# Query projections in 64-row halves beside scores in block 0, in cycles of three pairs, and the output weight's parts in DRAM

## The chip, the cores and the metric

The kernel runs on one core of a Trainium2 chip. The time is that of one launch on the device in microseconds (us); three runs of the kernel before gave 1419.66 to 1421.75, median 1420.86. The engines that matter here: PE (TensorE, matrix products), ACT (ScalarE, the exponentials), DVE (VectorE, elementwise work, and copies out of PSUM), POOL (GpSimd, weight preparation) and SP (SyncE, which issues most DMAs). Each works through a queue of its own in program order, and semaphores join them.

## What is computed

One transformer block on x of 2048 tokens by 512. There are 32 query heads of 16 columns that share one key and one value head; the feed-forward part has 1792 hidden columns.

```python
q = ln(x) @ wq                    # 32 heads of 16
k, v = ln(x) @ wk, ln(x) @ wv     # one head of 16
p = softmax(q @ k.T * 16**-0.5)   # each head: 2048 x 2048
h = x + concat_heads(p @ v) @ wo
h2 = h + (gelu(ln(h) @ w_gate) * (ln(h) @ w_up)) @ w_down
```

Every product with a weight is made of three products of split operands: high part by high part, low by high, high by low.

## The kernel before

Tokens are worked in four **blocks** of 512 (b = 0 to 3). In a block, eight **groups** of four heads (g) run over 16 **key chunks** of 128 keys (kc). The unit of the loop is a **pair** n: two heads of one key chunk. Two pairs make a chunk, 32 pairs a group, 256 pairs a block.

For a pair, `scores` (L361) issues two matmuls, one on the upper and one on the lower half of PE's rows (50 rows used in each: the query's high and low parts, and a bound for the exponent), into a score buffer `s` of two PSUM banks, and one exp of 128x1024 on ACT (L372). Three score buffers rotate in the stage in question, so pair n can't be scored before the exp of pair n-3 is done. When both pairs of a chunk have their exps, `weigh` (L374) multiplies the four heads' probabilities by v and a column of ones, in four column tiles of 32 (16 MATMUL rows of the trace are two chunks), into one accumulator `acc`. After 16 chunks `evacuate` (L387) copies it to SBUF on DVE (`oT`, L389), stores it to DRAM (`acc_d`, L393) and loads it back in another layout (`oc`, four DMAs, L402). When two groups are back, DVE takes reciprocals, divides, and splits the result into `o_hi` and `o_lo` (L414 to L433). Those steps wait in a list, `outs`, and `take_out` (L383) issues one entry of it now and then. In block 0 four empty entries are put ahead of them, so that they come later; with the last group of the block all entries are issued at once.

While block 0's scores run, the queries of the later blocks are still to be projected. `project_q` (L184) makes a block's queries in four parts c of 128 columns: 12 matmuls of 128x128x512 (L194) into `pq`, which has one buffer. DVE then reads `pq` for `qh` and `ql` (L116, L117), SP stores them to `q_d`, from which `load_q` (L349) takes each group's queries some time ahead. A block's last part is followed by four small matmuls for the squared norms (`pqn`, L232), and two steps on DVE (L236, L237). From these `factors` (`mm`, L242 to L251, on POOL) and `bound` (`m`, L258 on DVE, then a DMA) make the bound. After the last block's, `check_bound` stores a few numbers to `b_d` (L1387).

POOL meanwhile prepares the weights in `part_weights` (L466): 46 steps of load, split into high and low part, and store to DRAM; wo's four steps leave their parts in SBUF instead (L474).

The order of all this is written out by hand, in the loop `while n < lead` (L1014 to L1042); `lead` is 272. Every fourth pair is preceded by one step of the projections (three matmuls, L1024 to L1027), then four pairs are complete and all chunks but the last two pairs' are weighed (`finish`, L1035), an entry of `outs` is taken (L1037) and a step of the weight parts (L1039). When the projections are done, one chunk is weighed after every second pair (L1030). SP and DVE keep the order of the program in this stretch.

At n = 256 the pools of the first stage are closed. At n = 260 the dense part of block 0 is primed (`dense(0)`, L575): two loads of x (`xb`, L583) and the first four weight loads (`w1`, 512 KB each, L528), whose memory was that of the first stage. From n = 272 on its matmuls are woven among the scores of block 1, the output projection first (`project`, in 64-row halves by `duo`, L548). That projection runs over c = 0 to 3, and the last, c = 3, needs the eighth group's result. Later blocks repeat this, and a tail (L691) ends the last.

Of the kernel before, what the change touches and what calls it, by code (L numbers as in the profile page):

```python
# [9 lines left out]
F32 = mybir.dt.float32  # L10
F32R = mybir.dt.float32r
# [24 lines left out]

HURRY = ((0, 3), (1, 0), (1, 1))
# [7 lines left out]
CUT, EDGE, GAP, HOLD = -1, -2, -3, -4  # L45
# [3 lines left out]
def kernel(  # L49
# [51 lines left out]
    wo_hi = const.tile([P, DC, D], F32R, name="wo_hi")  # L101
    wo_lo = const.tile([P, DC, D], F32R, name="wo_lo")
# [7 lines left out]
    w2_d = dram.tile([FC, P, 2, D], F32R, name="w2_d")  # L110

# [43 lines left out]
    def run(outer, first):  # L155
# [28 lines left out]
        def project_q(b, cs, eng, col):  # L184
# [4 lines left out]
            for c in cs:  # L189
                pq = psum1(f"pq_{b}_{c}")  # L190
                n = 0
                for d in range(DC):
                    for wt, xt in ((wq_hi, xT_hi), (wq_hi, xT_lo), (wq_lo, xT_hi)):
                        nc.tensor.matmul(  # L194
                            pq, wt[:, d, c * P : (c + 1) * P], xt[:, d, :],
                            start=(n == 0), stop=(n == 3 * DC - 1),
                        )
                        n += 1
                    if urgent or d < DC - 1:
                        yield 3  # L200
# [72 lines left out]
            yield 2  # L273
# [19 lines left out]

        def later_products():
            second = project_q(1, range(DC), nc.vector, 1)
# [4 lines left out]
            for _ in range(2 * DC - sum(RAMP.values())):  # L300
                yield next(second)
            yield from q_rest
            yield from second
            for b in range(2, NB):
                yield from project_q(b, range(DC), nc.vector, b)

        def first_q():

            qg = eb.tile([P, 2, T], F32R, name="qg_first")
            view = q_d.rearrange("(u a) r s -> a r u s", a=2)  # L310
# [264 lines left out]
        def dense(b, tail=False):  # L575
# [15 lines left out]
            if b == 0:  # L591
                yield 0
# [872 lines left out]
```

## Time and profile before

| | |
|---|---|
| median of three runs | 1420.86 us (1419.66 to 1421.75) |
| the profiled execution | 1419.23 us, of which the profile's span is 1417.5 us |
| granted TensorE clock, mean | 0.998 |
| first exp of pair n = 32 / 256 / 271 | 85.69 / 307.55 / 321.30 us |
| first matmul of the output projection (`pp`) | 323.26 us |

Times in the profile count from the start of its span. Two executions differ by some tenths of a per cent, so terms that are worked out from the trace are put on the profiled execution's own time, and the median stands beside it. In a row of a time line, the first number is the start, the second the length, then engine, line of the program, operation, result, sources, shapes and count; in brackets stands the engine's idle time before it, and whose work ended that. Matmul rows overlap: the start of the next one tells when PE went on.

### The profile page before, as it was taken

The numbers are of one execution on the slowest core, as the hardware profiler recorded it, in microseconds if no ns is written. First come the engines' busy times: TensorE is split into PE (matmuls) and PEld (weight loads), VectorE is DVE, ScalarE is ACT, GpSimd is POOL, SyncE is SP. The second block draws the span as 40 slices with busy tenths as digits, with TensorE's granted clock in tenths as the row PEclk, the third lists the DMA queues.
The fourth block names the chain that finished last, engine by engine and source line by source line (L and its number), as shares of the span: only waits on it lengthen the run. The fifth ranks groups of instructions, "written<-read, shape, count | busy, mean of one in ns | idle before, by whom it ended". The sixth has DMA issues, their size and how long they took to land.

```text
span 1417.5 us, 25266 instructions
## 1 busy us (share of the span) xinstructions
PE 1401.8 (99%) x10502; PEld 786.5 (55%) x10502; DVE 542.6 (38%) x964; ACT 1041.4 (73%) x1149; POOL 228.7 (16%) x326
## 2 busy tenths in 40 slices
PE   9999999999999999999999999999999999999998
PEld 7533333224555655555555655655565556557886
DVE  7421223204352332514252332413443342427665
ACT  7699999997787787777777777877778777772000
POOL 6466776731000000000000000000000000002000
PEclk9999999999999999999999999999999999999999
DMA  4456766633242242213252232203243241433551
GB/s 159 154 190 210 231 220 217 221 126 114 82 150 91 88 144 84 90 41 114 94 165 82 97 135 82 92 23 123 89 144 116 87 146 38 141 126 134 177 206 65
DMA packets 66850, 180.31 MB, mean 127 GB/s; under 512 B 9484, under 2 KB 9484, under 8 KB 66696
## 3 DMA queue, kind: packets, MB, share of 16 engines
q1 hardware_dynamic: 56800, 144.43, 30.0%
q0 software_dynamic: 9760, 34.08, 7.3%
q8 instruction: 84, 1.38, 0.4%
q14 instruction: 38, 0.31, 0.1%
q10 hardware_dynamic: 168, 0.10, 0.0%
HBM read 130.87 MB, written 47.45 MB: 126 GB/s over the span
## 4 chain that ended last, share of the span: by engine, by line
PE 91%; ACT 6%; DMA 1%; issue 1%; DVE 0%; POOL 0%; SPq 0%; ACTq 0%; DVEq 0%; POOLq 0%
PE acc L376 31%; PE s L368 20%; PE pu L883 10%; PE pg L883 8%; ACT p L372 6%; PE pd L883 4%; PE pq L194 3%; PE pd L548 3%; PE pg L570 3%; PE pd L570 3%; PE pu L570 3%; PE pp L548 2%; DMA x<-in_A_x_dram 1%; PE pp L691 1%; PE pxt L623 1%
## 5 line engine op out<-in xcount | busy, mean ns | idle before, releaser
L372 ACT ACTIVATE p<-s 128x1024 f32<-128x1024 f32 x1024 | 970.1, 1054 | 234.4 <-PE s L368 232.8
L376 PE MATMUL acc<-p,v_sb 128*32 128x512 f32 x4096 | 488.3, 598 | 0.1
L368 PE MATMUL s<-qg,kaug 50*128 50x512 f32 x1984 | 396.0, 430 | 4.5 <-ACT p L372 4.3
L368 PEld LDWEIGHTS s<-qg,kaug 50*128 50x128 f32 x1984 | 175.1, 184 | 256.4 <-ACT p L372 160.0
L376 PEld LDWEIGHTS acc<-p,v_sb 128*32 128x32 f32 x4096 | 111.8, 109 | 227.3 <-issue 224.4
L883 PE MATMUL pu<-x2h,w 64*128 64x512 f32 x672 | 211.8, 391 | 0.0
L883 PE MATMUL pg<-x2h,w 64*128 64x512 f32 x672 | 211.4, 391 | 0.0
L883 PEld LDWEIGHTS pu<-x2h,w 64*128 64x128 f32 x672 | 116.2, 186 | 15.5
L883 PEld LDWEIGHTS pg<-x2h,w 64*128 64x128 f32 x672 | 116.4, 186 | 12.5 <-issue 0.3
L883 PE MATMUL pg<-x2l,w 64*128 64x512 f32 x336 | 122.2, 391 | 0.0
L883 PE MATMUL pu<-x2l,w 64*128 64x512 f32 x336 | 122.0, 390 | 0.0
L126 POOL TENSOR_SCALAR rstd<-mv 128x1 f32<-128x1 f32 x16 | 3.5, 221 | 685.3 <-DVE mv L124 685.2
L760 ACT ACTIVATE ga<-ga 128x512 f32<-128x512 f32 x56 | 35.3, 634 | 88.7 <-DVE ga L755 88.7
L883 PE MATMUL pd<-w,gh 64*128 64x512 f32 x384 | 81.3, 392 | 0.0
L389 DVE COPY oT<-acc 128x512 f32<-128x512 f32 x32 | 22.1, 692 | 142.1 <-PE acc L376 142.0
L825 DVE TENSOR_TENSOR h<-h,pd 128x512 f32<-128x512 f32 x48 | 31.9, 685 | 115.2 <-PE pd L883 66.3
L1092 DVE SCALAR_TENSOR_TENSOR ga<-ga,g 128x512 f32<-128x512 f32 x70 | 48.3, 690 | 52.2 <-ACT ga L760 51.1
L416 DVE RECIPROCAL oc<-oc 128x128 f32<-128x128 f32 x64 | 56.3, 921 | 30.1 <-DMA oc<-acc_d 11.3
L744 DVE COPY g<-pg 128x512 f32<-128x512 f32 x56 | 38.7, 692 | 63.2 <-PE pg L883 57.5
L883 PEld LDWEIGHTS pu<-x2l,w 64*128 64x128 f32 x336 | 58.2, 186 | 7.7
L883 PEld LDWEIGHTS pg<-x2l,w 64*128 64x128 f32 x336 | 58.2, 186 | 6.0
L757 DVE TENSOR_TENSOR g<-g,pu 128x512 f32<-128x512 f32 x56 | 38.3, 683 | 40.1 <-PE pu L883 30.2
(260 smaller groups left out, 1412.1 us busy)
## 6 DMA issues: line engine op xcount, KB each, us to landing
w<-w_d SPq DMA_DIRECT2D x112, 512.0 KB
w<-w_d SPq DMA_DIRECT2D x28, 1024.0 KB
qg<-q_d SPq DMA_DIRECT2D x62, 200.0 KB
q_d<-qh SPq DMA_DIRECT2D x32, 256.0 KB
acc_d<-oT SPq DMA_DIRECT2D x31, 256.0 KB
oc<-acc_d SPq DMA_DIRECT2D x124, 64.0 KB
w_d<-w_0b POOLq DMA_DIRECT2D x14, 512.0 KB, 5.6
w_d<-w_1b POOLq DMA_DIRECT2D x14, 512.0 KB, 4.5
```

What stands on the lines that cost most here:

```text
L194: nc.tensor.matmul(pq, wt[:, d, c * P : (c + 1) * P], xt[:, d, :], start=(n == 0), stop=(n == 3 * DC - 1),)
L368: nc.tensor.matmul(s[:, a, :], kaug[rows, kc * P : (kc + 1) * P], qg[rows, u, :], start=True, stop=True,)
L372: nc.scalar.activation(p[:, 2 * u : 2 * u + 2, :], s, AF.Exp, scale=SCALE)
L376: nc.tensor.matmul(acc[32 * j : 32 * j + 32, :], v_sb[:, kc, :], p[:, j, :], start=(kc == 0), stop=(kc == KC - 1), skip_group_check=True,)
L416: nc.vector.reciprocal(oc[:, 1, sl], oc[:, 1, sl])
L548: nc.tensor.matmul(banks[k], lhsT[rows], rhs[rows], start=(turn == 0 and i == 0), stop=(turn == 1 and i == n - 1), skip_group_check=True,)
L570: nc.tensor.matmul(bank, lhsT, rhs, start=(i == 0), stop=(i == len(ts) - 1))
L744: nc.vector.tensor_copy(g, pg)
L757: nc.vector.tensor_tensor(g, g, pu, op=ALU.mult)
L760: nc.scalar.activation(a, a, AF.Tanh, scale=GELU_A * GELU_C)
L883: nc.tensor.matmul(e["bank"], lhsT[rows], rhs[rows], start=i == 0 and not e["both"], stop=last and e["both"], skip_group_check=True,)
L1092: (soon or lazy).pop(0)()
```

## The change

- **Projections.** Parts c = 2 and 3 of block 1's queries and all of blocks 2 and 3 (ten parts) are projected in 64-row halves: 24 matmuls of 64x128x512 in place of 12 of 128 rows, 12 on the upper rows and then 12 on the lower, with a copy of one column of `pq` on DVE (`mark`) between. Each half is issued right ahead of a score matmul that uses the other 64 rows. A pair of scores takes two halves, and its two scores then lie on the same rows, one behind the other. For that each group of block 0 loads the queries of all four heads to both row halves (400 KB instead of 200 KB in each of two DMAs).
- **Cycles.** The first 32 pairs keep the old loop. From n = 32 to 272 there are 80 cycles of three pairs. Halves go with the second pair of a cycle, or with the second and the third, by the counts 4, 2, 4, 2, 4, 4, 4 for each part, which makes its 24. After each block's parts a cycle without halves holds `pqn`. A cycle ends with the weighing of all chunks that were complete before its third pair, which is one or two, then `take_out`, and on four of seven cycles a step of the weight parts. The projections end at n = 250 (192 before). `outs` gets six empty entries instead of four.
- **Order at the end of block 0.** The priming of `dense(0)` is issued inside a cycle, after pair 259, and before the weighing that completes the eighth group. So on SP the bound's store, `b_d`, xb, w1 and two new loads of wo come ahead of the eighth group's `acc_d` and `oc`; before, `acc_d` and `oc` came first.
- **wo.** Its parts are no longer kept in SBUF. POOL stores them to `wo_d`, with four more stores. `load_wo` brings them back for each block in two DMAs of 1 MB into buffers of w2: for block 0 in the priming, behind w1; for the next blocks ahead of the last down products.

```diff
--- before
+++ after
@@ -181,23 +182,37 @@
             k2m = eb.tile([H, 1], F32, name="k2m")
-        def project_q(b, cs, eng, col):
+        def project_q(b, cs, eng, col, halves=()):
             tsl = slice(b * T, (b + 1) * T)
             xT_hi, xT_lo = xT[b]
             urgent = b == 0 and cs[0] == 0
             qss = []
             for c in cs:
                 pq = psum1(f"pq_{b}_{c}")
-                n = 0
-                for d in range(DC):
-                    for wt, xt in ((wq_hi, xT_hi), (wq_hi, xT_lo), (wq_lo, xT_hi)):
+                terms = [
+                    (wt[:, d, c * P : (c + 1) * P], xt[:, d, :])
+                    for d in range(DC)
+                    for wt, xt in ((wq_hi, xT_hi), (wq_hi, xT_lo), (wq_lo, xT_hi))
+                ]
+                if c in halves:
+                    for a in range(2):
+                        rows = slice(64 * a, 64 * a + 64)
+                        for n, (lhsT, rhs) in enumerate(terms):
+                            yield a, partial(
+                                nc.tensor.matmul, pq, lhsT[rows], rhs[rows],
+                                start=(a == 0 and n == 0),
+                                stop=(a == 1 and n == len(terms) - 1), skip_group_check=True,
+                            )
+                        if a == 0:
+                            mark = eb.tile([P, 1], F32, tag="qmark", bufs=2, name=f"mark_{b}_{c}")
+                            nc.vector.tensor_copy(mark, pq[:, :1])
+                else:
+                    for n, (lhsT, rhs) in enumerate(terms):
                         nc.tensor.matmul(
-                            pq, wt[:, d, c * P : (c + 1) * P], xt[:, d, :],
-                            start=(n == 0), stop=(n == 3 * DC - 1),
+                            pq, lhsT, rhs, start=(n == 0), stop=(n == len(terms) - 1)
                         )
-                        n += 1
-                    if urgent or d < DC - 1:
-                        yield 3
+                        if n % 3 == 2 and (urgent or n < len(terms) - 1):
+                            yield 3
                 raw = None
                 if (b, c) in HURRY:
...
@@ -224,9 +239,11 @@
                         q_d[c * HC : (c + 1) * HC, r0 : r0 + DH, tsl].bitcast(F32),
                         part.bitcast(F32),
                     )
-                if raw is None or b == 0:
+                if c not in halves and (raw is None or b == 0):
                     yield 3
+            if halves:
+                yield REST
             pn = psum1(f"pqn_{b}_{cs[0]}")[:H, :]
             for i, c in enumerate(cs):
                 nc.tensor.matmul(
...
@@ -278,41 +296,40 @@
         q_first = project_q(0, range(FIRST_Q), nc.scalar, 0)
         q_rest = project_q(0, range(FIRST_Q, DC), nc.scalar, NB)
-        def later_q():
-            for said in later_products():
-                for entry in after:
-                    entry[0] -= 1
-                while after and after[0][0] <= 0:
-                    after.pop(0)[1]()
-                yield said
-            while after:
-                yield 0
-                after.pop(0)[1]()
-                yield 0
-            check_bound(eb, k2m)
-        def later_products():
-            second = project_q(1, range(DC), nc.vector, 1)
+        def early_q():
+            second = project_q(1, range(DC), nc.vector, 1, range(FULL_Q, DC))
             for _ in range(sum(RAMP.values())):
                 yield next(second)
             next(q_rest)
-            for _ in range(2 * DC - sum(RAMP.values())):
+            for _ in range(FULL_Q * DC - sum(RAMP.values())):
                 yield next(second)
             yield from q_rest
-            yield from second
-            for b in range(2, NB):
-                yield from project_q(b, range(DC), nc.vector, b)
+            rest_q.append(second)
+            rest_q.extend(project_q(b, range(DC), nc.vector, b, range(DC)) for b in range(2, NB))
+        rest_q = []
+        def half_q():
+            for gen in rest_q:
+                yield from gen
+        def age():
+            for entry in after:
+                entry[0] -= 1
+            while after and after[0][0] <= 0:
+                after.pop(0)[1]()
...
@@ -347,26 +364,32 @@
         sb = outer.enter_context(tc.tile_pool(name="attn", bufs=1, side="right"))
         def load_q(b, g):
-            qg = sb.tile([P, 2, T], F32R, tag="qg", bufs=2, name=f"qg_{b}_{g}")
-            view = q_d.rearrange("(u a) r s -> a r u s", a=2)
+            qg = sb.tile([P, 4, T], F32R, tag="qg", bufs=2, name=f"qg_{b}_{g}")
+            view = q_d.rearrange("h r s -> r h s")
             for a in range(2):
+                hs = slice(0, 4) if b == 0 else slice(a, 4, 2)
                 nc.sync.dma_start(
-                    qg[64 * a : 64 * a + KR, :, :].bitcast(F32),
-                    view[a, :, 2 * g : 2 * g + 2, b * T : (b + 1) * T].bitcast(F32),
+                    qg[64 * a : 64 * a + KR, hs, :].bitcast(F32),
+                    view[:, 4 * g : 4 * g + 4, b * T : (b + 1) * T][:, hs, :].bitcast(F32),
                 )
             return qg
         o_blk, pair, outs, last_out = {}, [None], [], []
-        def scores(i, p, qg, kc, u):
+        def scores(i, p, qg, kc, u, beside=()):
             third = width == 1 and (2 * i + u) % 3 == 2
             pool, tag, bufs = (ps, "s3", 1) if third else (pss, "s", 2)
             s = pool.tile([P, 2, T], F32, tag=tag, bufs=bufs, name=f"s_{i}_{u}")
             for a in range(2):
-                rows = slice(64 * a, 64 * a + KR)
+                row = 64 * a
+                if beside:
+                    lane, step = beside[a]
+                    row = 64 * (1 - lane)
+                    step()
+                rows = slice(row, row + KR)
                 nc.tensor.matmul(
-                    s[:, a, :], kaug[rows, kc * P : (kc + 1) * P], qg[rows, u, :],
+                    s[:, a, :], kaug[rows, kc * P : (kc + 1) * P], qg[rows, 2 * u + a, :],
                     start=True, stop=True,
                 )
             nc.scalar.activation(p[:, 2 * u : 2 * u + 2, :], s, AF.Exp, scale=SCALE)
...
@@ -450,7 +473,7 @@
                 last_out.extend([piece, gather])
             elif k == 1:
-                outs.extend([[] for _ in range(4 if b == 0 else 1)])
+                outs.extend([[] for _ in range(6 if b == 0 else 1)])
                 outs.extend([partial(invert, t), partial(invert, t + 1)] for t in (0, 2))
                 outs.append([divide, high, low])
             if b == 0 and g == NG - 1:
...
@@ -492,11 +507,15 @@
                     both.rearrange("p i (c n) -> p i c n", c=DC).bitcast(F32),
                 )
-            def store_2(f, both):
-                nc.gpsimd.dma_start(w2_d[f].bitcast(F32), both.bitcast(F32))
+            def store_2(dst, both):
+                nc.gpsimd.dma_start(dst.bitcast(F32), both.bitcast(F32))
             steps = [
-                (partial(load_wo, c), partial(part_wo, c), None) for c in range(DC)
+                (
+                    partial(load_f, wo_t[:, c : c + 1, :], f"wo{c}"),
+                    partial(part_f, f"wo{c}", False), partial(store_2, wo_d[c]),
+                )
+                for c in range(DC)
             ]
             for f in range(FC):
                 fs = slice(f * P, (f + 1) * P)
...
@@ -534,6 +553,26 @@
                 w.bitcast(F32), w2_d[2 * j : 2 * j + 2].rearrange("f p i d -> p f i d").bitcast(F32)
             )
             return w[:, :, 0], w[:, :, 1]
+        def load_wo(b):
+            for j in range(DC // 2):
+                w = db.tile([P, 2, 2, D], F32R, tag="w2", bufs=W2, name=f"wo_{b}_{j}")
+                nc.sync.dma_start(
+                    w.bitcast(F32),
+                    wo_d[2 * j : 2 * j + 2].rearrange("c p i d -> p c i d").bitcast(F32),
+                )
+                wos[b, 2 * j], wos[b, 2 * j + 1] = w[:, 0], w[:, 1]
+        wos = {}
+        def out_terms(b, t, cs):
+            o_hi, o_lo = o_blk[b]
+            return [
+                (ot[:, c, t * P : (t + 1) * P], wos[b, c][:, k, :])
+                for c in cs
+                for ot, k in ((o_hi, 0), (o_hi, 1), (o_lo, 0))
+            ]
         def duo(names, terms):
...
@@ -943,6 +971,7 @@
             if not tail:
                 yield from weave(plan)
                 yield from down(RUNS[-2], False)
+                load_wo(b + 1)
             yield from down(RUNS[-1], True)
         PER = NG * KC
...
@@ -1007,39 +1036,68 @@
         with tc.manual_schedule(engines={mybir.EngineType.SP, mybir.EngineType.DVE}):
             parts, said = None, 3
             if first:
-                work = later_q()
+                work = early_q()
                 parts = part_weights(early.enter_context(tc.tile_pool(name="parts", bufs=1)))
-            while n < lead:
-                if n == 2 * PER:
-                    drain()
-                    for _ in parts or ():
-                        pass
-                    parts = None
-                    early.close()
-                    db = late.enter_context(tc.tile_pool(name="dense", bufs=1))
-                if n % 4 == 0:
-                    given = work is not None and said > 0
-                for _ in range(RAMP.get(n, n > 7 and n % 4 == 3) if work is not None else 0):
-                    said = next(work, 0)
-                    if said == 0 and not after:
-                        drain()
+            while n < 2 * KC:
+                for _ in range(RAMP.get(n, n > 7 and n % 4 == 3) if first else 0):
+                    next(work, 0)
+                    age()
                 score(n)
                 n += 1
-                if n % 4 == 2 and not given and len(pend) > 2:
-                    finish(1)
                 if n % 4:
                     continue
                 if len(pend) > 2:
                     finish(len(pend) - 2)
+                if parts is not None and n > 12 and n % 24:
+                    next(parts, None)
+            token, counts = None, iter(())
+            if first:
+                drain()
+                work = half_q()
+                token = next(work)
+                counts = (k for _ in range(NB * DC) for k in (4, 2, 4, 2, 4, 4, 4))
+            for cycle in range((lead - n) // 3):
+                age()
+                rest = token == REST
+                count = next(counts) if token is not None and not rest else 0
+                for j in range(3):
+                    if n == 2 * PER:
+                        assert token is None
+                        for _ in parts or ():
+                            pass
+                        while after:
+                            age()
+                        if first:
+                            check_bound(eb, k2m)
+                        parts = work = None
+                        early.close()
+                        db = late.enter_context(tc.tile_pool(name="dense", bufs=1))
+                    if 0 < j <= count // 2:
+                        score(n, (token, next(work)))
+                        if j < count // 2:
+                            token = next(work)
+                    else:
+                        score(n)
+                    n += 1
+                    if n == 2 * PER + 4:
+                        primed = dense(0)
+                        next(primed)
+                if rest:
+                    token = next(work, None)
+                ready = [e[2] for e in pend if e[5] < n - 2]
+                if KC - 1 in ready:
+                    ready = ready[: ready.index(KC - 1) + 1]
+                finish(len(ready))
+                if count:
+                    token = next(work, None)
                 if outs:
                     take_out()
-                if parts is not None and n > 12 and n % 24:
+                if parts is not None and cycle % 7 % 2 == 0:
                     next(parts, None)
-                if n == 2 * PER + 4:
-                    primed = dense(0)
-                    next(primed)
+            assert n == lead
         assert not outs
         work = primed
         set_banks("ps_rest")
```

More of the change, by code (lines that the diff above doesn't have):

```diff
@@ L35 @@
 FIRST_Q = 1
+FULL_Q = 2
 HURRY = ((0, 3), (1, 0), (1, 1))
@@ L272, in project_q @@
             after.extend([[2, factors], [4, bound]])
-            yield 2
+            if not halves:
+                yield 2
         after = []
@@ L520, in part_weights @@
                 both = part(raws.pop(i))
-                left = None if store is None else partial(store, both)
+                left = partial(store, both)
                 yield 1
@@ L975, in run, with score @@
         cur = {}
-        def score(n):
+        def score(n, beside=()):
             nonlocal acc
@@ L990, in score @@
                 cur["p"] = sb.tile([P, 4, T], F32, tag="p", bufs=PB, name=f"p_{i}")
-            scores(i, cur["p"], cur["qg"], kc, u)
+            scores(i, cur["p"], cur["qg"], kc, u, beside)
             if u == 1:
```

40 lines of the change are left out of this document (11 added, 29 removed).

## The prediction, made before the run

> **What bounds the kernel now.** I read the page's busy shares and its chain of waits first.
>
> ```profile
> PE 1401.8 (99%) x10502; PEld 786.5 (55%) x10502; DVE 542.6 (38%) x964; ACT 1041.4 (73%) x1149; POOL 228.7 (16%) x326
> ...
> PE 91%; ACT 6%; DMA 1%; issue 1%; DVE 0%; POOL 0%; SPq 0%; ACTq 0%; DVEq 0%; POOLq 0%
> ```
>
> TensorE is busy 99% of the span and carries 91% of the chain, so what the change does to block 0 stays in the time unless the later blocks have room for it; PE at 99% gives them none. ScalarE's 73% is a mean over stages. The changed stage is block 0, from pair n=32 to n=271 (a pair is one exp of 128x1024 and its two score matmuls). So next come the busy times by stretches of 32 pairs, cut at the exps' starts (span, then PE, PEld, DVE, ACT, POOL busy).
>
> ```profile
> 85.70:118.33 32.63, 32.63 (x221) 12.44 (x217) 6.93 (x10) 30.18 (x33) 23.70 (x31) 1.00 0.65 222
> ...
> 216.50:249.09 32.59, 32.45 (x219) 12.41 (x217) 7.18 (x10) 30.18 (x33) 21.39 (x25) 1.00 0.66 218
> 249.09:278.43 29.34, 28.45 (x195) 8.19 (x191) 6.96 (x11) 29.15 (x33) 23.15 (x30) 1.00 0.67 215
> 278.43:307.55 29.12, 29.12 (x194) 8.48 (x192) 0.69 (x1) 29.12 (x33) 15.89 (x19) 1.00 0.47 159
> 307.55:321.30 13.75, 13.75 (x94) 3.87 (x92) 3.53 (x5) 13.75 (x17) 0.00 (x0) 1.00 0.40 131
> ```
>
> With a projection in it, a stretch takes 32.6 us (five of them, the first and the last shown, 163.4 us in all). Without, it takes 29.12, with ACT busy throughout: 0.91 us for each exp, ACT's own pace. So 224 pairs take 221.9 us where ACT alone needs 224 x 0.91 = 203.8. **The loss is 18 us**, and all that the projections' new place can win. Where it arises is seen in one cycle, on PE and on ACT.
>
> ```profile
> 150.29 0.98 PE L368 MATMUL s<-qg,kaug 50*128 50x512 f32 x6
> 151.20 0.50 PE L194 MATMUL pq<-xT_hi,wq_hi 128*128 128x512 f32 x1
> 151.54 0.40 PE L194 MATMUL pq<-xT_lo,wq_hi 128*128 128x512 f32 x1
> 151.77 0.39 PE L194 MATMUL pq<-xT_hi,wq_lo 128*128 128x512 f32 x1
> 152.09 0.50 PE L368 MATMUL s<-qg,kaug 50*128 50x512 f32 x2
> 152.52 1.92 PE L376 MATMUL acc<-p,v_sb 128*32 128x512 f32 x16
> 154.37 0.97 PE L368 MATMUL s<-qg,kaug 50*128 50x512 f32 x6
> ```
>
> ```profile
> 150.93 3.77 ACT L372 ACTIVATE p<-s 128x1024 f32<-128x1024 f32 x4 [0.33 <-PE s L368]
> 154.98 1.02 ACT L372 ACTIVATE p<-s 128x1024 f32<-128x1024 f32 x1 [0.28 <-PE s L368]
> ```
>
> Three score buffers rotate, so the cycle's fourth pair may start only when the first pair's exp has ended (150.93 + 1.02 = 151.95); the projection stands ahead of it until 152.09. Behind it on PE come 0.43 to the weighing (152.52), 1.85 for the weighing of two key chunks (154.37), and 0.61 to the next exp (154.98). That is longer than the three exps in hand last, and ACT stands still 0.28. From exp to exp the cycle is 4.05 us against 4 x 0.91 = 3.64: 0.41 lost per cycle of four pairs, 40 times.
>
> **The change, part by part.** First TensorE's own time. Three projection matmuls take 152.09 - 151.20 = 0.89 us, and leave two changes of tile shape around them. Six halves beside scores give three more slots. A slot's price is seen where the output projection already runs in 64-row halves among scores; the same rows say when block 0's first result is needed.
>
> ```profile
> 323.26 0.39 PE L548 MATMUL pp<-wo_hi,o_hi 64*128 64x512 f32 x2
> ...
> 325.81 0.40 PE L548 MATMUL pp<-wo_hi,o_hi 64*128 64x512 f32 x2
> ```
>
> Between these starts lie eleven slots (of pp and of s): 2.55 / 11 = 0.232 us. Three cost 0.70 instead of 0.89, some 0.2 saved per step and 8 us over the 40 steps, if PE set the pace. The Trainium skill ("TensorEngine Tiling (Array Packing)", Key Properties) says that a change of tiling mode drains TensorE; the trace agrees, as the first projection matmul lasts until 0.34 after its start, the one inside the group 0.23. By that rule alone the time would fall by these 8 us.
>
> But ACT's loss arises in the wait above, so I work that out for the new cycle of three pairs. The last pair waits for the exp of the last pair of the cycle before. From that exp's start t: 1.02 for the exp, 0.05 to the score (an estimate; it lies between 0 and the 0.14 from 151.95 to 152.09), one slot of 0.23 more if the pair carries halves, 0.43, the weighing, 0.61. With two chunks weighed (1.85) the next cycle's first exp starts at t + 4.19, or t + 3.96 without halves; ACT would be ready after four exps of 0.91, at t + 3.64. So 0.55 or 0.32 is lost. With one chunk (half, 0.93) the sum is 3.27 and nothing is lost, but with three buffers nothing is stored either: the next cycle loses the same again. Three pairs make one and a half chunks, so cycles weigh one and two by turns. Counted in the changed instruction order up to n=251: of 38 cycles with two chunks, 27 have halves on the last pair (counts of 4) and 11 don't; 36 weigh one. Loss 27 x 0.55 + 11 x 0.32 = 18.4 us. The old loss was 18. **The same loss, for projections that now last to n=250** instead of 192.
>
> Second, DVE. Its order is fixed, and at three places the copy of a finished accumulator (L389) now stands ahead of a finished projection's qh and ql or of the mark: after groups 2, 3 and 6.
>
> ```profile
> 242.13 0.69 DVE L116 CAST qh<-pq 128x512 fp32r<-128x512 f32 x1 [13.84 <-PE pq L194]
> ```
>
> pq has one buffer. Behind oT (0.69, below) qh and ql take 0.69 each, so the next half waits about 2.0 us, and the score that comes behind it on PE too. Less the exps in hand, my step-by-step sum over the order (which gives the times of before to 0.3 us) puts ACT's loss at 1.6, 0.9 and 2.3: **4.8 us**, estimated. Bounds: nothing (the score buffers cover it) and 3 x 2.0 = 6.
>
> Block 0 then: 18.4 + 4.8 = 23.2 lost against 18.1, **+5.1 us** (between -2 and +9, from 0.1 more or less per cycle and the bounds of the waits).
>
> Third, the end of block 0 and its loads. First what stands there before, on DVE and on SP's queue.
>
> ```profile
> 310.73 0.69 DVE L389 COPY oT<-acc 128x512 f32<-128x512 f32 x1 [28.64 <-PE acc L376]
> 318.47 3.39 DVE L416 RECIPROCAL oc<-oc 128x128 f32<-128x128 f32 x4 [7.04 <-DMA xb<-in_A_x_dram]
> ...
> 322.61 0.43 DVE L427 CAST o_hi<-oc 128x512 fp32r<-128x512 f32 x1
> ```
>
> ```profile
> 311.45 0.35 SPq L393 DMA_DIRECT2D acc_d<-oT  x1
> 313.55 1.91 SPq L402 DMA_DIRECT2D oc<-acc_d  x4
> 315.84 1.57 SPq L583 DMA_DIRECT2D xb<-in_A_x_dram  x2
> 317.46 2.11 SPq L528 DMA_DIRECT2D w<-w_d  x4
> 319.67 1.02 SPq L353 DMA_DIRECT2D qg<-q_d  x2
> ```
>
> The last accumulator goes out and comes back ahead of the loads; o_hi is ready at 323.04, and the first matmul that needs its last quarter is the pp of 325.81: 2.8 us of room. In the changed order acc_d and oc stand behind b_d (the bound's store), xb, w1 and two new 1 MB loads of wo. And xb waits for b_d to land and for POOL's last store, behind mm_3. That hangs on the last projection, whose steps before are these (pqn on PE; norms on DVE; mm on POOL; m on DVE; b_d on SP):
>
> ```profile
> 245.21 1.04 PE L232 MATMUL pqn<-qs,sel 128*32 128x512 bf16 x4
> ```
>
> ```profile
> 246.28 0.68 DVE L236 COPY qn<-pqn 32x512 f32<-32x512 f32 x1 [2.03 <-PE pqn L232]
> 246.99 0.68 DVE L237 TENSOR_REDUCE q<-qn 32x1 f32<-32x512 f32 x1
> ```
>
> ```profile
> 260.42 0.26 POOL L242 TENSOR_SCALAR mm<-q,k2m 32x1 f32<-32x1 f32 x1
> ```
>
> ```profile
> 262.07 0.54 DVE L258 TENSOR_SCALAR m<-qn,mm 32x512 fp32r<-32x512 f32 x1 [8.80 <-POOL mm L251]
> ```
>
> ```profile
> 263.02 0.42 SPq L1387 DMA_DIRECT2D b_d<-q2m  x1
> ```
>
> The last norms' matmuls (pqn) follow the scores of n=250. By the losses above exp 250 starts at about 306.6, so its score, released by the end of exp 247, at 306.6 - 3 x 0.91 + 1.02 = 304.9. A slot and 1.04 of pqn make 306.2; the norms take 246.99 + 0.68 - 246.28 = 1.4, to 307.6; 263.02 - 260.42 = 2.6 more to b_d's issue at 310.2; 2.1 to its landing (acc_d to oc above, 311.45 to 313.55). POOL's last store follows mm_3 and lands beside it. So xb is issued at **some 312.5 to 313**, 3 us earlier than before, but now w1, wo, acc_d and oc stand behind it on SP, and 4.5 MB ahead of acc_d in the queues (the qg behind them is for a group not needed before n=288). What such loads take:
>
> ```profile
> GB/s 400 66 0 0 0 0 0 0 0 0 20 213 16 148 98 213 269 304 335 390 415 386 195 155 26 0 0 0 15 0 0 0 22 300 144 0 0 0 0 0
> ```
>
> This is 300 to 345 us in 40 slices. xb and w1 (2.5 MB) take some 9 us from 315.84 on; at the plateau of 0.4 MB/us, the 2 MB of wo add 5: 14 us, to 327. Does acc_d queue behind them? A case of it, and a quiet one (the second fence is DVE's):
>
> ```profile
> 387.13 0.32 SPq L393 DMA_DIRECT2D acc_d<-oT  x1
> 390.26 1.72 SPq L402 DMA_DIRECT2D oc<-acc_d  x4
> ...
> 629.47 0.35 SPq L393 DMA_DIRECT2D acc_d<-oT  x1
> ```
>
> ```profile
> 635.22 0.95 DVE L416 RECIPROCAL oc<-oc 128x128 f32<-128x128 f32 x1 [1.01 <-DMA oc<-acc_d]
> ```
>
> Behind a 1 MB load oc's issue came 3.1 us after acc_d's, quiet 2.1: it queues. The Trainium skill ("DMA: Bandwidth & Descriptors", Queues, rings and completion order) says that each DMA engine takes the descriptors of a ring in order; the trace agrees with that extra 1.0 us. So acc_d lands at 327.6, the reciprocal follows 5.75 - 2.1 = 3.6 later at 331.2, o_hi ends 323.04 - 318.47 = 4.6 behind that: 335.8. PE, shifted by 5.1, wants it at 330.9. **It stalls 4.9 us** (between 0, if the transfers don't queue, and 8). wo lands before 327 and is used from 328.4: no wait.
>
> The rest I take at nothing: POOL's four more stores lie beside its parts, which end at 299 before (below); the second half of qg (200 KB per group more) is loaded a group ahead; later loads of wo are issued during the last down products, several us before use. Without that cover, a 2 MB load costs 5 us at each of three ends.
>
> Sum on the profiled execution: 1419.23 (span 1417.5) + 5.1 + 4.9 = 1429.2. The median shown is 1.6 above the profiled time, so **1431**.
>
> **Rivals.**
> 1. It does what it says: halves hide, ACT keeps 0.91. Then pair 271 comes 18 us earlier. But the load chain takes over:
>
> ```profile
> 298.89 0.63 POOL L496 DMA_DIRECT2D w_d<-w213b  x1 [0.30 <-POOL w213b L117]
> ```
>
> POOL's last store at about 301 with four stores more, landed by 303.4; loads to 317.4, o_hi at 326.2 against 325.81 before: 1419.6 profiled, **1421**, no change. It decides once block 0 loses under some 14 us instead of 23 (the 9.6 between 303.4 and 313). For it speaks the saved 8 us on PE; against it that ACT's wait holds two chunks and 0.61 with no projection in them. Chance 0.09.
> 2. As 1, and acc_d does not queue: wo still lands only at 317 and is wanted at 307, so PE gives back 10 of the 18: **1412**, faster. Against it stands 390.26. Chance 0.06.
> 3. Only block 0 slips, the end of it is covered: **1426**. Chance 0.20, on the forecast's side.
> 4. More half waits, slower loads: both upper bounds, +9 and +8, **1438**. Chance 0.10.
>
> The forecast keeps 0.55. **Range**: 1421 (rival 1) to 1438; it leaves out rival 2 and the tails. A measurement tells 0.2% (2.8 us) from no change; so faster 0.07 (rival 2 and a little), same 0.09, slower 0.84.
>
> **What would show it.** In the changed profile: exps 32 to 256 spread over 225 to 229 us with ACT gaps of about 0.3 to 0.45 after every second cycle; a longer gap near n=99, 134 and 228, PE ended by DVE qh; xb issued near 313; acc_d behind four w and two wo loads; PE idle some 5 us in pp, ended by DVE o_hi. Wrong would make it: no ACT gaps in cycles of two chunks, acc_d landing within 3 us of its issue, or parts on POOL that end after 309.

## The result, and the profile after

The changed kernel takes 1439.61 us (median of four runs, 1437.67 to 1441.21) against 1420.74 before: a ratio of 1.0132, 95% interval 1.0115 to 1.0150. It is slower by 18.9 us, where 10 were forecast, and lies 1.6 us above the forecast's range.

The page of the changed kernel, busy shares and the chain of waits:

```profile
PE 1400.2 (98%) x10622; PEld 787.2 (55%) x10622; DVE 541.4 (38%) x974; ACT 1042.7 (73%) x1149; POOL 231.9 (16%) x330
...
PE 87%; ACT 6%; DMA 2%; DVE 2%; issue 1%; SPq 1%; POOL 1%; ACTq 0%; DVEq 0%; POOLq 0%
```

PE's share of the chain falls from 91% to 87%, and what takes its place are DMA, DVE, SP's queue and POOL: a chain off PE now ends later than PE's own work. The profiled execution (1437.67, span 1436.0) says where. The two traces side by side, by starts:

| point | before | after | later by |
|---|---|---|---|
| exp 32 | 85.69 | 85.45 | -0.2 |
| exp 271 | 321.28 | 325.22 | 3.9 |
| first pp of the output projection | 323.26 | 329.15 | 5.9 |
| first pp with the last quarter of o_hi | 325.81 | 340.79 | 15.0 |
| exp 288 | 346.08 | 362.34 | 16.3 |
| exp 1023 | 1275.36 | 1293.05 | 17.7 |
| span | 1417.5 | 1436.0 | 18.5 |

Block 0 gives 3.9 us, and **12.3 us fall between exps 271 and 288** (24.80 before, 37.12 after), at the join of block 0's attention and its output projection. First SP's queue there (DMA issues):

```profile
308.67 0.35 SPq L279 DMA_DIRECT2D q_d<-m  x1
309.11 0.37 SPq L1445 DMA_DIRECT2D b_d<-q2m  x1
314.74 0.82 SPq L621 DMA_DIRECT2D xb<-in_A_x_dram  x2
315.62 3.11 SPq L547 DMA_DIRECT2D w<-w_d  x4
318.77 1.14 SPq L561 DMA_DIRECT2D wo<-wo_d  x2
320.01 0.46 SPq L416 DMA_DIRECT2D acc_d<-oT  x1
332.47 1.75 SPq L425 DMA_DIRECT2D oc<-acc_d  x4
```

acc_d is issued at 320.01, and oc, which waits for it to land, at 332.47: 12.5 us for a transfer whose follower came 2.1 us later before. Two pieces of the chain of work that ended last, with their lengths, name the DMAs that xb and oc waited for:

```profile
309.11 4.91 DMA b_d<-q2m
...
320.01 12.44 DMA acc_d<-oT
```

DVE and PE in the same stretch:

```profile
313.86 0.69 DVE L412 COPY oT<-acc 128x512 f32<-128x512 f32 x1 [4.97 <-PE acc L399]
336.16 3.39 DVE L439 RECIPROCAL oc<-oc 128x128 f32<-128x128 f32 x4 [21.61 <-DMA oc<-acc_d]
...
340.31 0.43 DVE L450 CAST o_hi<-oc 128x512 fp32r<-128x512 f32 x1
```

```profile
329.15 1.22 PE L587 MATMUL pp<-wo,o_hi 64*128 64x512 f32 x4 [2.32 <-DMA wo<-wo_d]
...
333.09 0.43 PE L391 MATMUL s<-qg,kaug 50*128 50x512 f32 x2
340.79 1.22 PE L587 MATMUL pp<-wo,o_hi 64*128 64x512 f32 x4 [7.28 <-DVE o_hi L450]
341.81 0.63 PE L391 MATMUL s<-qg,kaug 50*128 50x512 f32 x2
342.23 0.63 PE L587 MATMUL pp<-wo,o_lo 64*128 64x512 f32 x2
```

The accumulator's copy is made at 313.86 and its result is usable at 340.7. PE waits twice, 2.32 us for wo and 7.28 for o_hi. And it runs slowly behind each wait: 341.81 to 342.23 is 0.42 us for a slot that took 0.23 before. The granted clock says the same (PEclk is the third number from the end, before the DMA engines' busy share and their GB/s):

```profile
325.22:330.00 4.78, 2.46 (x16) 1.18 (x10) 0.00 (x0) 3.00 (x4) 0.00 (x0) 0.90 0.99 385
330.00:335.00 5.00, 3.51 (x20) 2.61 (x18) 0.00 (x0) 1.97 (x2) 0.00 (x0) 0.75 0.20 58
335.00:340.00 5.00, 0.00 (x0) 0.00 (x0) 3.81 (x5) 0.00 (x0) 0.00 (x0) 0.59 0.29 90
340.00:345.00 5.00, 4.21 (x22) 1.97 (x26) 1.55 (x4) 1.94 (x2) 0.00 (x0) 0.50 0.00 0
345.00:350.00 5.00, 5.00 (x42) 2.75 (x36) 0.00 (x0) 2.03 (x3) 0.00 (x0) 0.88 0.02 3
```

So PE's 12.32 are: 1.95 for wo (5.89 - 3.94), 7.28 for o_hi, and 3.09 that are left, put down to the lower clock: 1.81 between the first pp and the wait for o_hi, 1.28 behind that wait. These are not separate costs. The 1.95 and the 1.81 lie ahead of the wait for o_hi, which would have been longer by as much without them: by o_hi alone PE stands 11.0 us late at 340.79 (325.81 + 3.94 = 329.75 would have been its time), and the 1.28 come on top.

### The profile page after: what moved, and what is told of

It reads as the page before. It is cut to its first block, busy times and chain, and to the rows that moved or that the text cites. A ratio compares the mean times of both kernels' runs of the same rounds, so it can differ in the third digit from the quotient of the medians.

```text
span 1436.0 us, 25546 instructions
## 1 busy us (share of the span) xinstructions
PE 1400.2 (98%) x10622; PEld 787.2 (55%) x10622; DVE 541.4 (38%) x974; ACT 1042.7 (73%) x1149; POOL 231.9 (16%) x330
## 4 chain that ended last, share of the span: by engine, by line
PE 87%; ACT 6%; DMA 2%; DVE 2%; issue 1%; SPq 1%; POOL 1%; ACTq 0%; DVEq 0%; POOLq 0%
PE acc L399 30%; PE s L391 19%; PE pu L911 9%; PE pg L911 8%; ACT p L395 6%; PE pd L911 5%; PE pd L587 3%; PE pd L609 3%; PE pg L609 3%; PE pu L609 3%; PE pp L587 2%; PE pq L389 1%; DMA acc_d<-oT 1%; PE pq L211 1%; PE pp L719 1%
## 5 line engine op out<-in xcount | busy, mean ns | idle before, releaser
L391 PE MATMUL s<-qg,kaug 50*128 50x512 f32 x1984 | 420.2, 426 | 7.6 <-ACT p L395 7.5
L391 PEld LDWEIGHTS s<-qg,kaug 50*128 50x128 f32 x1984 | 192.4, 184 | 254.4 <-ACT p L395 126.5
```

Of the source, the lines that this page charges most:

```text
L391: nc.tensor.matmul(s[:, a, :], kaug[rows, kc * P : (kc + 1) * P], qg[rows, 2 * u + a, :], start=True, stop=True,)
```

## The experiments

Theory A: the join makes most of the loss, because acc_d queues behind xb, w1 and wo. Theory D: block 0's loss beyond the cycles' own comes from DVE's order. Theory L: the cycles' own loss is the wait worked out in the prediction, so it depends on where the halves stand and not on their number. Rivals: the halves and cycles themselves cost it; or the added 2 MB do, in any order. The kernel before had medians of 1420.59, 1420.60 and 1420.16 us in the three groups of runs below.

**prime_late**: the priming behind the weighing.

```diff
-                    if n == 2 * PER + 4:
-                        primed = dense(0)
-                        next(primed)
...
                 finish(len(ready))
+                if n == 2 * PER + 4:
+                    primed = dense(0)
+                    next(primed)
```

> The changed kernel, but block 0's dense part is primed behind the weighing that ends its eighth group, so that acc_d and oc stand ahead of xb, w1 and wo on SP, as before the change; halves, cycles and wo in DRAM stay. Theory A (the chain at the end: of the 18.4 us between the two profiled executions 3.9 lie in block 0 and 12.4 between n=271 and n=288, because acc_d queues behind 4.5 MB): o_hi's last quarter is in time, the last in line is now wo, issued at about 320 and landed at about 331 to 333 where the first pp wants it at 327; PE stands 4 to 6 us in pp, ended by the DMA of wo, and loses 1 to 2 us more at a lower granted clock. Median 1430 (1427 to 1433). Rival B (the halves or the cycles cost it, the wait only shows it): within 3 us of the changed kernel's 1439.6.

1433.96 us, ratio 1.0088 (1.0072 to 1.0105). That is 1 us above the range expected, and outside rival B's. The reciprocals come at 324.35, and PE no longer waits for o_hi. Its long wait is one, for wo, as theory A has it; from PE's waits between 300 and 350 us (total, times, longest):

```profile
PE pp L587 <- DMA wo<-wo_d: 5.8, 1, 5.8
```

**prime_late_wo_first**: in addition `load_wo(0)` ahead of `load_x(0)`.

> As prime_late, and the two loads of wo come ahead of xb and w1. Theory A: wo lands at about 323 to 326, before pp wants it; nothing is left but block 0's 3.9 us and at most 2 us in the later blocks: median 1424.5 to 1427; exp 288 at 349.5 to 351. Rival C (the 2 MB more cost their transfer time in any order, 5 us): 1430 or more, with PE idle in pp or later for w1 or xb.

1426.98 us, ratio 1.0043 (1.0026 to 1.0060). PE waits neither for wo nor for o_hi; exp 288 is at 352.23, later than the 349.5 to 351 expected, since block 0 ended at 328.24 in this execution. 12.6 of the 18.9 us are gone by the order of seven DMAs (acc_d, four oc, two wo), with all 4.5 MB still loaded: the rival of the volume falls.

**wo_first**: only `load_wo(0)` ahead of `load_x(0)`, acc_d behind all loads.

> The changed kernel with the two loads of wo ahead of xb and w1, and the priming where the change put it, so that acc_d still stands behind all of the loads. Theory A: PE's wait for wo (2.3 us) goes, and o_hi's last quarter comes as late as before, near 340.7, so that the wait for it grows by as much: 1438 to 1440.5, no gain that can be told. If the two waits are separate costs: 1436 to 1437.

1439.06 us, ratio 1.0127 (1.0110 to 1.0144): nothing gained. The wait for wo is gone, the wait for o_hi is longer. SP, then PE:

```profile
323.36 0.33 SPq L416 DMA_DIRECT2D acc_d<-oT  x1
335.01 1.73 SPq L425 DMA_DIRECT2D oc<-acc_d  x4
```

```profile
343.43 1.22 PE L587 MATMUL pp<-wo,o_hi 64*128 64x512 f32 x4 [10.43 <-DVE o_hi L450]
```

So the two waits are not separate costs: o_hi ends last, and what PE waits for earlier is waited for anyway.

**before_wo_in_dram**: the kernel before with wo's parts in DRAM alone (the four stores, `load_wo` and `out_terms` of the change).

> The kernel before with only wo's parts moved to DRAM: four more stores by POOL, two loads of 1 MB for each block, for block 0 behind xb and w1 (acc_d and oc stay ahead). Theory A: exps up to n=271 as before (321.3); wo lands at about 328 to 331, wanted from 323.3 on: PE idle 5 to 7 us in pp, ended by the DMA of wo, and 1 to 2 us at a lower clock; 1427 to 1430. If such loads are hidden, as the prediction took them for the changed kernel: 1420.7, within 1. A shift that grows by more than 0.5 us at the ends of blocks 1 and 2 would be the price of the later loads of wo.

1430.11 us, 0.1 above the range expected, ratio 1.0062 (1.0045 to 1.0079). PE's long wait between 300 and 350 us:

```profile
PE pp L563 <- DMA wo<-wo_d: 7.0, 1, 7.0
```

The wo part costs 9.5 us by itself where it is loaded last, with acc_d ahead and no halves at all. Across the ends of blocks 1 and 2 the shift against the kernel before grows by 0.1 (exps 500 to 544) and 0.2 us (exps 700 to 800): no price of the later loads of wo shows.

**change_wo_kept**: the change without its wo part. The room comes from four buffers of p instead of five and 4 KB for the first group's queries (`PB = 4`, `qg_first` as before).

> The changed kernel without its wo part: wo's parts stay in SBUF (four buffers of p, a first group's queries of 4 KB), so that only xb and w1, 2.5 MB, stand ahead of acc_d. Theory A: acc_d lands some 5 us earlier than behind 4.5 MB; o_hi's last quarter is 2 to 4 us late instead of 7 to 10, the wait for wo is gone: median 1429 to 1434. If the order alone made the loss: within 2 of 1439.6.

1433.13 us, ratio 1.0090 (1.0075 to 1.0106). Behind 2.5 MB instead of 4.5 acc_d needs 8.3 us:

```profile
318.46 1.09 SPq L418 DMA_DIRECT2D acc_d<-oT  x1
326.77 1.73 SPq L427 DMA_DIRECT2D oc<-acc_d  x4
```

PE waits 5.6 us for o_hi, more than the 2 to 4 I expected; the time is in the range. Two thirds of the loss stay without any load of wo; the order alone, in prime_late_wo_first, took off two thirds with all of wo loaded. So the order weighs more than the volume. This run also has a buffer of p less, which no run takes by itself.

**change_again**: the changed kernel, one more execution.

> The changed kernel once more, to see whether block 0 ends at 325.2 (its first profile) or at 328.2 as in prime_late, prime_late_wo_first and wo_first, which have the same order on PE up to n=256. If the difference is whether PE's clock drops behind the two waits for ql, the profile shows the losses at n=101 and 230 at 1.5 and 1.9, or at 0.1 and 0.9, and nothing in between that is new.

1439.56 us, one run. Exp 271 comes at 328.25, as in the three variants with the same order, not at 325.22 as in the first profile. From exp to exp, the loss against 0.91 at n=99, 101, 228 and 230 is 1.45, 1.57, 1.60 and 2.02; in the first profile 1.43, 0.06, 1.13 and 0.92. This execution lies at the changed kernel's median, the first profile 1.9 us below it; its shift against the kernel before is 7.0 us up to exp 271, 11.4 at the join and 2.1 behind it. At n=99 PE and DVE of the first profile show the place:

```profile
150.97 0.50 PE L391 MATMUL s<-qg,kaug 50*128 50x512 f32 x2
153.17 0.49 PE L389 MATMUL pq<-xT_hi,wq_hi 64*128 64x512 f32 x1 [1.70 <-DVE ql L118]
```

```profile
151.11 0.69 DVE L412 COPY oT<-acc 128x512 f32<-128x512 f32 x1 [5.26 <-PE acc L399]
151.71 0.68 DVE L117 CAST qh<-pq 128x512 fp32r<-128x512 f32 x1
152.43 0.69 DVE L118 TENSOR_TENSOR ql<-pq,qh 128x512 fp32r<-128x512 f32 x1
```

oT stands ahead of qh and ql, and the half waits 1.70 us for ql. The second loss comes behind it. The stretches before and after the wait, first of the changed kernel's first profile, then of prime_late_wo_first (same instructions):

```profile
149.10:153.16 4.06, 2.37 (x19) 0.60 (x18) 2.02 (x4) 3.08 (x4) 3.56 (x6) 1.00 0.68 236
153.16:156.64 3.48, 3.47 (x28) 1.67 (x32) 0.96 (x1) 2.70 (x3) 3.10 (x4) 1.00 0.82 255
```

```profile
149.10:153.16 4.06, 2.36 (x19) 0.60 (x18) 2.03 (x4) 3.06 (x4) 3.64 (x5) 1.00 0.64 204
153.16:156.64 3.48, 3.48 (x18) 1.03 (x18) 0.64 (x1) 1.94 (x2) 2.40 (x4) 0.57 0.82 233
```

The same wait, and behind it a clock of 1.00 in one execution and 0.57 in the other: 28 matmul rows done in 3.48 us, or 18. What differs is told in the last section.

**q_first**: prime_late_wo_first with qh and ql ahead of oT.

```diff
+                if count:
+                    token = next(work, None)
                 ready = [e[2] for e in pend if e[5] < n - 2]
...
-                if count:
-                    token = next(work, None)
```

> As prime_late_wo_first, but a finished projection's qh and ql are issued on DVE ahead of the copy of the accumulator (oT) where both fall into one cycle. Theory D (DVE's order): the half that waits for ql no longer waits 1.7 us, and PE no longer drops to its lower clock behind that wait; the ACT losses at n=99 and 101 (3.0 us) and 228 and 230 (3.6, of which 0.6 stays) go: exp 271 at 322.0 to 323.2 in place of 328.2, median 1420.5 to 1422.5 (1427.0). Rival (the losses come from the change of row half or from pq's one buffer, whatever stands on DVE): within 1.5 us of 1427.

1422.12 us (10 runs), ratio 1.0012 (1.0003 to 1.0022); exp 271 at 322.24. At the place above, DVE and PE now read:

```profile
149.70 0.69 DVE L118 TENSOR_TENSOR ql<-pq,qh 128x512 fp32r<-128x512 f32 x1
150.31 1.18 DVE L233 TENSOR_TENSOR qs<-qh 128x512 bf16<-128x512 f32 x1
151.41 0.68 DVE L412 COPY oT<-acc 128x512 f32<-128x512 f32 x1
```

```profile
150.95 0.50 PE L391 MATMUL s<-qg,kaug 50*128 50x512 f32 x2
151.29 0.40 PE L389 MATMUL pq<-xT_hi,wq_hi 64*128 64x512 f32 x1
```

The half follows the score after 0.34, without a wait. All four extra losses are gone: theory D holds, the rival falls. The 1.5 us left against the kernel before are what halves, cycles and wo in DRAM still cost together in this arrangement.

**change_q_first**: the same edit on the changed kernel, priming and loads as there.

> The changed kernel with DVE's order alone put right (qh and ql ahead of oT); loads and priming as in the change. If the terms add: block 0 ends at 322.2 instead of 325.2 to 328.2, the end's wait stays (acc_d behind 4.5 MB, 12 us): median 1433 to 1437. If block 0's slip were covered by the later wait for o_hi anyway: no change from 1439.6, within 1.5.

1435.33 us, ratio 1.0111 (1.0095 to 1.0127): 4.3 us off, and exp 271 at 322.14. PE still waits 2.7 us for wo and 6.9 for o_hi. The terms add; the chain behind acc_d moves with block 0's end, since the loads hang on the last projection.

**free_places**: four halves in every cycle, placed by the chunks to be weighed (a part's first cycle keeps its last two pairs); pqn only in a cycle of one chunk; later blocks' bounds six cycles later. From the edit:

```diff
+                coming = [e[2] for e in pend] + [n // 2 % KC] * (n % 2)
...
+                    places = (0, 1) if len(coming) > 1 and done % 24 else (1, 2)
...
-                    if 0 < j <= count // 2:
+                    if j in places:
```

> As q_first, with the halves moved to where the cycle's sum leaves room: four in every cycle, on its first two pairs if it weighs two chunks, on its last two if it weighs one; the four pqn matmuls only in a cycle of one chunk; the bound of a block some cycles later. Theory L (a cycle loses what stands between the last pair's score and the next exp beyond 3.64 us): cycles of two chunks lose 0.3 instead of 0.57, and the projections end 20 pairs earlier: exp 271 at 319.5 to 321, median 1418 to 1420.5. Rival (the loss is PE's work in all, wherever it stands): no earlier than q_first.

1419.97 us (10 runs), ratio 0.9997 (0.9988 to 1.0007): not to be told from the kernel before. Exp 271 comes at 318.67, a little earlier than expected. ACT in steady cycles, first of the changed kernel, then of free_places:

```profile
194.83 5.61 ACT L395 ACTIVATE p<-s 128x1024 f32<-128x1024 f32 x6 [0.42 <-PE s L391]
200.63 4.69 ACT L395 ACTIVATE p<-s 128x1024 f32<-128x1024 f32 x5 [0.20 <-PE s L391]
```

```profile
191.38 5.61 ACT L395 ACTIVATE p<-s 128x1024 f32<-128x1024 f32 x6 [0.19 <-PE s L391]
197.18 5.61 ACT L395 ACTIVATE p<-s 128x1024 f32<-128x1024 f32 x6 [0.19 <-PE s L391]
```

Six exps, two cycles, then a gap: 0.42 where the last pair carried halves, 0.2 where it didn't. (The loss is some 0.15 more than the gap, as a row ends when its last exp ends.) Theory L holds.

**free_places_two_pairs**: cycles of two pairs and one chunk once the projections are through.

> As free_places, and once the projections are through, cycles of two pairs with one chunk each, as the kernel before has them there. Theory L: the last 40 pairs lose nothing: exp 271 at 318 to 320, median 1417 to 1419.5. Rival as for free_places.

1420.05 us (10 runs), ratio 0.9999 (0.9989 to 1.0008), no further gain, and above the range expected. The profiled execution has no loss from n=242 on, as expected, but 3.0 us at n=230, where PE waits 1.0 for oT and its clock is at 0.50 from 278.7 to 282.1. What it would bring without that stays open.

**wo_kept_four_p** and **free_places_wo_kept**: the last two with wo kept in SBUF, as in change_wo_kept.

> As free_places_two_pairs, but wo's parts stay in SBUF as in the kernel before, no wo loads at all; the room comes from four buffers of p instead of five and from a first group's queries of 4 KB. If the loads of wo cost what the later blocks showed (1 to 3 us from n=288 to the end, in prime_late_wo_first and before_wo_in_dram): 1415 to 1417.5. If four buffers of p bind, ACT gains idle time in all blocks, and the median comes out above free_places_two_pairs.

> free_places (cycles of three pairs to the end) with wo kept in SBUF and four buffers of p. The gains add: block 0 ends at 318 to 319 and the later blocks lose nothing to loads of wo: 1416 to 1418, below the kernel before by 0.2% or a little more. If five buffers of p are needed: above 1419.

1417.54 us (10 runs), ratio 0.9980 (0.9971 to 0.9990), and 1416.81 us (9 runs), ratio 0.9974 (0.9964 to 0.9984). Both beat the kernel before, by 0.20% and 0.26%, the first at the edge of its expected range, the second within. The second's profile, of the slowest of its nine runs, doesn't show the block 0 that was expected: it has the loss at n=230 too (3.15 us, again with the clock at 0.50), and exp 271 at 321.50. The change's idea holds its promise only there: halves beside scores, in the places that are free, with the loads out of the way.

## Why the prediction was wrong

**The step that failed is "It stalls 4.9 us (between 0, if the transfers don't queue, and 8)".** Its mechanism was right: acc_d queues behind the loads, and o_hi ends last. Its size was not. o_hi held PE up by 11.0 us, beyond the bound of 8, and the join cost 12.3. From 4.9 to 12.3:

- *The loads' start, 1.7.* I took 2.1 us for the landing of b_d, from acc_d's. Its own was 4.9 (309.11 to 314.02), in the kernel before too (263.02 to 267.91), which I could have read there. So xb was issued at 314.74, 1.7 us after my 313, though block 0 ended earlier than forecast. The profile's list of waits puts this one down to q_d<-m, done at 313.84; but in the five executions that prime ahead of the weighing (the change twice, wo_first, change_wo_kept, change_q_first) the first load follows the end of b_d by 0.72 us each time, and that of q_d<-m by 0.9 to 2.7.
- *The loads' length, 3.1.* From xb to the landing of acc_d I had 14.6 us (313 to 327.6); it took 17.7 (314.74 to 332.45). The plateau of 0.4 MB/us was right (385 GB/s in the stretch above). Of acc_d's 16 completions 15 came by 330.7 and the last at 332.4: that one makes 1.7 of the 3.1. From oc's issue to the reciprocal the forecast 3.6 was 3.7.
- *Block 0, 1.2.* It slipped by 3.9 us, not by 5.1, so PE wanted o_hi 1.2 us earlier, and waited for it so much longer.
- *The clock, 1.3.* I had no term for it: PE's loss behind the wait for o_hi, put down to the granted 0.50 there. The 1.8 us that it lost ahead of that wait cost nothing more. The Trainium skill ("TensorE: Matmul & The Clock Gate", Part 1: The HAM clock gate) says that an idle window of about 3.4 us puts the array on half its clock, until it was busy as long. The 7.3 us wait and the 0.50 behind it agree; the 1.70 us wait with 0.57 behind it, above, and the 2.32 us wait for wo, with 0.50 behind it (last section), do not, as they are shorter.

*wo.* "wo lands before 327 and is used from 328.4: no wait" was wrong by the same lateness: 2.3 us. wo_first shows that this wait hides in the next.

**Block 0** was right in its parts. Cycles of two chunks lose 0.58 with halves on the last pair and 0.35 without (0.55 and 0.32 forecast), cycles of one chunk lose nothing. q_first, where nothing else is left, loses 19.0 us from exp 32 to 256 against 18.4 by the cycles, and 18.0 in the kernel before. So the 64-row halves bring nothing as they are placed here: shown by free_places, which moves them (with pqn and the later bounds) and wins 3.6 us at exp 271. DVE's term, 4.8 us within 0 to 6, came out at 2.9 in the first profile and 6.1 in the second, just above its bound (225.76 and 228.88 us between the same exps, against 222.82 in q_first). It fell on groups 2 and 6, not on 3, where the mark did not wait; its size depends on whether the clock drops behind the wait. So +5.1 forecast stood against +3.9 and +7.0.

**"The rest I take at nothing"**: 2.2 us more arise between exp 288 and the end. Part of it may be that the profiled execution of before lies 1.5 us below its median. q_first, with wo in DRAM, is longer by the same 2.2 there, and change_wo_kept, without any load of wo, by 2.3: so the later loads of wo are not shown to cost anything. What the remainder is stays open.

**The rivals.** Rival 4 (both upper bounds, 1438) came nearest in time, and by slower loads, as it says; but the join cost 12.3, more than its +8, and block 0 less than its +9. Rival 2 fell: acc_d queues in every variant that puts it behind the loads. Rival 3 (block 0 slips, its end is covered, 1426) is not the change, but it is what prime_late_wo_first made of it: 1427. Rival 1 (no loss on ACT) was seen in no variant, and its floor, the load chain behind POOL's last store, was not reached: change_q_first still gained all of what block 0 gained. That floor was itself priced too early: POOL's last store was issued at 308.0 in the changed kernel, not at 301.

## What to carry to other kernels

When a step is moved in a hand-written order, list the DMAs it issues and ask which small, urgent transfer now stands behind them: seven DMAs in another order were worth 12.6 us, more than all that the halves were meant to save on PE (8 us by the prediction's sum). Price a DMA's landing by that DMA's own row, not by another's. Price a wait on PE at its length plus the slow stretch that can follow it. And when a loop's period is set by a wait (three score buffers), extra work is free only in the places that the wait's sum leaves free, so write that sum for each kind of cycle before placing it.

## What the runs showed of the hardware

- PE's granted clock fell to about half behind a wait of only 1.70 us in prime_late_wo_first (0.57 in the next 3.48 us), and not in the changed kernel's first profile (1.00) behind the same wait. So the same kernel differs by some 3 us between executions (exp 271 at 325.22 and 328.25).
- The clock's record holds only 1.00 and 0.50 in all of these traces. Apart from the first and the last stretch of an execution it changes on a grid of 3.41 us: its stretches at 0.50 last 3.41, 6.83, 10.24 or 13.65 us. The rows at 0.75 and 0.57 are means over such stretches. The join in the first profile of the changed kernel, cut at the grid:

```profile
329.10:332.49 3.39, 3.34 (x16) 2.90 (x18) 0.00 (x0) 0.00 (x0) 0.00 (x0) 0.50 0.29 111
332.51:335.90 3.39, 1.00 (x8) 0.50 (x6) 0.00 (x0) 1.97 (x2) 0.00 (x0) 1.00 0.38 98
335.93:346.15 10.22, 5.36 (x26) 2.29 (x30) 5.36 (x8) 1.94 (x2) 0.00 (x0) 0.50 0.09 32
```

- Where a wait falls on that grid goes with whether the clock drops. Six executions have two waits of 1.70 us for ql each. Eight of these twelve lie within one step of the grid (one of them but for 0.07 us), and a step at 0.50 follows each; four lie across a border of it (in the first profile at 151.60, counted back from 329.09), and the clock stays at 1.00. No run moves the grid alone, so this is a match and not a proof; and the 1.0 us wait at n=230, in a step with 1.4 us idle in all, was followed by 0.50 too.
- A store of 64 KB (q_d<-m) took 5.2 us to its last completion. Of its 16 completions, 15 came within 2.8 us of the issue; the last came 2.4 us behind them. A store of 128 bytes (b_d) took 4.9 in the same trace.
